# Attention outputs of batches two to four: transposed by TensorE into free PSUM columns instead of by DMA

## The chip, the cores and the metric

The kernel runs on one core of one Trainium2 chip. The metric is the device time of one execution in microseconds; lower is better. The engines of the core are TensorE (PE, with its weight loads PEld), VectorE (DVE), ScalarE (ACT), GpSimd (POOL) and SyncE (SP, which here only issues DMAs). Each works through its own queue in order and waits on semaphores for the others. TensorE writes to PSUM (here four cells of 128 partitions by 1024 float32 values), the others read it from there.

## The reference

A block-sparse attention (four batches, eight heads, 768 positions, head width 64) is followed by a two-layer network on every token.

```python
scores = scale * np.matmul(q, k.transpose(0, 1, 3, 2))
mask = np.abs(blk_i - blk_j) <= window            # blocks of 32, window 1
mask = mask | (blk_i == 0) | (blk_j == 0) | (blk_i == n_blocks - 1) | (blk_j == n_blocks - 1)
for qb in range(n_blocks):
    for kb in sampled_blocks[qb]:                 # three sampled blocks for each block of queries
        mask[qb * block:(qb + 1) * block, kb * block:(kb + 1) * block] = True
attn = softmax(np.where(mask, scores, -1e9))
x = np.matmul(attn, v)        # then heads side by side: 3072 tokens x 512
h = x @ w_in                  # 512 x 2048
r = np.maximum(h, 0.0)
out = (r * r) @ w_out         # 2048 x 512
```

(The softmax is written out in the reference; it is shortened here.)

## The kernel before, in words

**Units and stages.** A unit `u` is a pair of heads of one batch (four units to a batch, `HP = 4`). Batches one and two (`SB = 2`) compute dense scores for tiles of 256 queries (`q0` is 0, 256 or 512), in three pairs of key chunks: `scores`, `exps`, `masks`, then `values` (or `values_full`), which leaves the unnormalized outputs and their sums in one PSUM cell, `otile`. Batches three and four gather only the key and value blocks that are needed. They go by six visits `v` of 128 queries, all four units at once: `s_scores`, `s_exps`, `s_masks`, and `s_values`, which leaves the outputs of all eight heads in one PSUM cell.

**From the outputs to the network.** `normalize` and `s_normalize` (VectorE: a reciprocal and a multiplication) write the outputs as bfloat16, with tokens on the partitions. The network's first matmul (`hidden`) needs them with features on the partitions, in a tile `xT` for each 256 tokens of a batch. Batch one takes the way over TensorE: `normalize` writes `xq`, `x_transp` transposes it by identity matmuls into columns 384 to 511 of the same PSUM cell, which the outputs leave free (`spare_of`), and `x_evac` copies that to `xT`. Batches two to four take the way over DMA: `normalize` and `s_normalize` write to the two-slot tile `XS`, and `x_transp_dma` (two transfers for a tile of batch two) and `s_transp` (one for a visit) issue transposing DMAs from SyncE that write `xT`. There the PSUM cell is given back after the normalization.

**The network.** For each of the twelve tiles of 256 tokens `hidden` is issued in four units `f` of four parts, then `relu` (ScalarE or VectorE) and `square` (ScalarE, GpSimd or VectorE), then eight parts of `output`, `out_copy` and `store`. Hidden and output matmuls of earlier tiles are interleaved with the attention of later ones.

**What sets the order.** `PROGRAM` is a list of words, one for each task, written out by hand or by a planner outside of the kernel: a letter for the engine (P, V, A, G, S), the task's number, and after a slash the PSUM cell of a task that takes one. Tasks are numbered in the order in which the code creates them, so a change in the number of tasks renumbers all later ones. `run_program` issues them in this order, and each engine's queue has its words in the order of the list. `get` and `put` name the buffers that a task takes and gives back. All matmul pairs are recorded at one line (203, in `pair`), and all copies at lines 121 and 123 (in `copy`), so the profile's groups are told apart by tiles and shapes.

Of the kernel before, what the change touches and what calls it, by code (L numbers as in the profile page):

```python
# [19 lines left out]
P = 128  # L20
# [5 lines left out]
def kernel(  # L26
# [11 lines left out]
    nc = tc.nc  # L38
# [12 lines left out]
    QW = 256  # L51
# [348 lines left out]
    def x_claim(b, q0, e):  # L400
        xs_at[0] += 2

    def normalize(u, q0, w, e):
        n = w // P
        po = outs_of(otile[u, q0], w)
        rs = work.tile([P, 2, 2, 1], F32, name="rs", tag="rs")[:, :, 0:n]
        V.reciprocal(out=rs, in_=po[:, :, :, D:VW])
        b, a = divmod(u, HP)
        xq = XS[:, :, a] if b else XQ[buf_of["xq", u, q0].at][:, 0:n]
        V.tensor_tensor(out=xq.rearrange("p c h d -> p h c d"), in0=po[:, :, :, 0:D], in1=rs.broadcast_to([P, 2, n, D]), op=AOP.mult)  # L410
        if not b:
            xtile[u, q0] = xq
        else:
            otile.pop((u, q0))
# [11 lines left out]
    def x_tile(b, c0):  # L426
        if (b, c0) not in xT:
            xT[b, c0] = XTT[xb[b, c0].at]
        return xT[b, c0]
# [4 lines left out]

    def x_transp_dma(b, q0, e):
        for c in range(2):
            sy.dma_start(out=x_tile(b, q0)[:, :, c * P:(c + 1) * P], in_=XS[:, c].rearrange("p a h d -> p (a h d)"), transpose=True)  # L437
# [214 lines left out]
    def s_normalize(b, v, e):  # L652
        po = otile.pop(("s", b, v))[:, :, 0:HP * VW].rearrange("p h (a d) -> p h a d", d=VW)
# [7 lines left out]
    def s_transp(b, v, e):  # L661
        sy.dma_start(out=x_tile(b, v // 2 * QW)[:, :, v % 2 * P:v % 2 * P + P], in_=xtile.pop(("s", b, v)).rearrange("p a h d -> p (a h d)"), transpose=True)
# [115 lines left out]
    def T_(f, *args, **kw):  # L778
        return Task((lambda e: f(*args, e)), **kw)
# [61 lines left out]
    def attend(a, add):  # L841
# [24 lines left out]
        by_dma = b > 0  # L866
        if by_dma:
            if (b, q0) not in x_of:
                xsb = [Buf("xs"), Buf("xs")]
                x_of[b, q0] = (T_(x_claim, b, q0, get=xsb), [], xsb)  # L870
            cl, nms, xsb = x_of[b, q0]
            nms.append(T_(normalize, u, q0, w, deps=[va, cl], put=[ob[u, q0], ot]))
            if len(nms) == HP:
                t = T_(x_transp_dma, b, q0, deps=nms + x_get(b, q0), put=xsb)
                mu.update({(b * HP + i, q0): t for i in range(HP)})
            return
# [5 lines left out]
    def visit(b, v, vw, acts):  # L882
# [28 lines left out]
        nm = T_(s_normalize, b, v, deps=[va], get=[xs], put=[yb, ot])  # L911
        mu["s", b, v] = T_(s_transp, b, v, deps=[nm] + x_get(b, v // 2 * QW), put=[xs])

    x_of = {}
# [46 lines left out]
    for T in TILES:  # L961
# [35 lines left out]
        V109 V153 V207 V332 V18 V19 V20 V28 V42 V53 V294 V29 A32 V35 P30/0 P36/1 P0/2 P33/3 V31 V37 A1 P11/0 V34 P100/1 G46 A101  # L997
        P47/0 P104/2 V43 A105 P44/3 P102/1 V45 V57 V48 A103 P58/2 V54 P111/3 V59 P55/0 A112 P113/2 V56 P115/1 V41 P4/0 A114 P9/3
        P125/0 V67 P2/3 A116 P106/2 V3 G52 G64 A126 P5/3 P123/1 V107 A124 P108 P65/3 G74 P121/0 V110 V66 P68/2 A122 V69 G63 P82/1
        P84/3 P131/2 V83 A85 P135/0 A132 P86/1 P117/3 G49 V87 A136 P10/2 G60 V118 G73 P61/1 P133/2 V62 P90/0 P119 G38 A134 P12/1  # L1000
        V120 V91 P168/1 G75 P15/3 P39/3 P174/0 A169 V40 P127/2 G76 A175 P137/3 G78 V128 P144/1 G70 V138 P129 P147/0 A145 V130 P139
        V176 P88/2 A89 V140 P71/1 V170 P171/3 A148 P779/2 V72 P780 V146 A172 P187/1 P92/0 P781 V93 A188 P782 V173 P50/3 P181/0 A783
        P177/1 V189 V51 A182 P141/2 V178 G784 P772/3 P773 A142 V149 P184/0 P179 P774 G79 G22 V180 A185 P94/2 P775 V143 P155/1 A95
        V776 G785 P150/0 A156 P158/2 V151 P161/3 A159 P786/1 V183 P152 P787 V186 A154 P215/2 A162 P788 V157 P14/0 P789 V160 A216
        P98/0 P190/3 S80 V163 A99 P212/2 V790 A778 P164/0 S251 S252 A213 V191 S81 P793/1 G791 A777 V165 P794 P209/2 P192 G792 P166
        P795 A210 V167 V193 P796 V217 S259 S260 P822/0 G77 V383 A797 P823 P197/3 P194/2 P824 V214 A198 G799 P825 P816/1 A195 V826
        P817 G254 P226/3 A798 P818 S255 V196 A227 P200/2 P810/0 V264 P811 A201 V211 S267 P243/3 P819 V256 S265 P812 A244 V228 P218/2
        V199 P813 A820 P219 P800/3 S257 A814 V220 V202 P240/1 P221 P801 A241 V262 S261 P96/0 S263 P802 A222 V97 A815 P237/1 V242
        P223/2 P203/0 A238 V245 P803 V272 A224 P229/1 P204 S268 P804 A230 V225 S275 S276 P805 A821 V231 S273 P286/2 G266 V205 P806
        A287 P232/1 V239 A827 P206 P289/2 P233 V270 P807 V208 A290 S271 V234 P296/0 A808 V291 P246/2 S253 P235 P247 V236 A297 V288  # L1010
        S437 P299/3 P828/1 V248 P829 A300 V280 P302/0 P830 V278 A303 P249 P283/3 V250 S279 V298 P831 A284 P314/2 P850/0 V832 V434
        S277 P851 A315 S281 P844/3 V304 P845 A833 V285 P311/1 P852 V258 A312 P853 V301 P846 S269 P847 A854 S21 V316 P292/2 V313
        P862/1 A848 P293 P305/0 V295 A855 P863 G282 P308/3 P306 G849 S454 A309 P864 S436 V307 P353/2 P865 A354 P326/3 P856/0 V866
        P857 A327 P320/2 P858 V274 A321 P323/1 V310 S438 P834/3 S445 V355 A324 P859 S444 V322 P347/2 S460 P835 V495 A860 V328 V325
        P317/1 A348 P350/0 P318 P836 S809 A351 V319 V349 P329/2 A867 P334/1 V352 P330 P837 V331 A335 V23 P356/0 S333 A861 P340/2
        P838 G447 A341 P839 G439 P362/1 G441 P357 P840 A363 G459 S452 P337/2 P841 S442 A338 G443 P868/1 G449 A842 V345 P359/2 P869
        S450 A360 P374/3 V342 P870 A375 V358 S446 P365/2 S440 V339 P377/3 A366 P871 V336 A378 V361 P343/0 S843 P371/2 V364 P344 S462
        P872 V367 A372 S448 V346 P368/3 V376 P398/2 P369 V373 A399 P873 S461 V379 S453 P380/0 V370 V469 P401/2 P381 A402 P385/3 V382
        P874 V400 A386 S384 P391/0 P388/2 V451 A392 V403 P16/3 P875 A389 P404/3 V876 P884/0 S612 P885 A405 P425/2 P886 V406 A426
        G463 P24/1 P887 V26 V25 P878/3 A888 P879 P428/2 G467 P880 S630 A429 P881 S468 V427 P407/0 V27 A882 S464 G465 P408 V396  # L1020
        P422/2 A889 V409 P924/1 G455 P925 A423 V457 P926 S456 P890/3 V387 A883 P927 V393 P891 A928 P413/0 V390 P892 P893 A414 S466
        P896/2 V894 P897 A929 P394/1 P898 V424 P395 P416/0 V397 P930/3 S458 A417 G470 A895 S614 P899 G472 P931 S604 V538 V900 P410/1
        S613 P932 A411 S471 P933 V430 P902/0 A934 V501 P475/2 P903 A476 A901 P912/1 V418 P904 V415 S620 V412 P431/3 V497 V540 V477
# [61 lines left out]
```

## Time and profile before

| | us |
|---|---|
| median of 3 runs (lowest, highest) | 256.85 (256.68, 257.36) |
| profiled execution | 254.29 |
| its span, first to last instruction | 252.5 |
| TensorE busy | 240.6 |
| ScalarE busy | 184.3 |
| VectorE busy | 166.0 |
| GpSimd busy | 93.6 |

"Busy" counts an engine's instructions, not its register, branch, semaphore and DMA-issuing ones. A matmul of the table lasts from its issue to its modelled end, and matmuls overlap, so the mean time of one matmul is not what it adds to the queue: that is seen from the start of one row of the timeline to the start of the next. In rows of groups the numbers after the bar are total busy time, mean nanoseconds of one, and idle time of the engine just before them, with what ended it. In rows of waits: total microseconds, times, and the longest. In rows of one line or tile the three durations are the shortest, the median and the longest in nanoseconds.

### The profile page before, as it was taken

Reading aid. Unit: us, or ns where it says so; the run is one execution under the profiler, and the core shown is the slowest. Engines: PE = TensorE matmul, PEld = TensorE weight load, DVE = VectorE, ACT = ScalarE, POOL = GpSimd, SP = SyncE. Lnnn points to the kernel's source line nnn. Section 1 sums busy time; section 2 is a strip of 40 time slices with the busy share of each in tenths; the row PEclk is TensorE's granted clock in tenths of the full one; section 3 lists DMA queues with packets and bytes.
Section 4 is the critical chain, followed back from the end, with each engine's and each line's share of the span. In section 5 each row is a group of like instructions: output and inputs, shape, how many; then the busy total and the mean of one; then the engine's idle time right before and its main releaser. Section 6 shows DMA issues by size and latency. Waiting matters only on the chain.

```text
span 252.5 us, 12042 instructions
## 1 busy us (share of the span) xinstructions
PE 240.6 (95%) x5265; PEld 179.0 (71%) x5265; DVE 166.0 (66%) x394; ACT 184.3 (73%) x216; POOL 93.6 (37%) x192
## 2 busy tenths in 40 slices
PE   7878999999999998999999999999999999999993
PEld 4646889768965677876866875867866765777683
DVE  7657997879789979685474876535566667641301
ACT  3978999999998889768758777768697465235340
POOL 3075525010407005329337982053806307060110
PEclk9999999999999999999999999999999999999999
DMA  6999999999999999995799999951835645242022
GB/s 194 365 243 181 204 188 278 221 275 182 272 280 195 160 253 308 181 248 135 223 301 178 223 238 204 286 132 34 258 56 86 159 125 142 65 127 83 3 86 86
DMA packets 63507, 47.08 MB, mean 186 GB/s; under 512 B 31455, under 2 KB 58464, under 8 KB 63456
## 3 DMA queue, kind: packets, MB, share of 16 engines
q1 hardware_dynamic: 58320, 37.61, 64.3%
q0 software_dynamic: 4448, 8.25, 16.0%
q8 instruction: 41, 0.67, 1.2%
q10 hardware_dynamic: 688, 0.46, 0.6%
q14 instruction: 10, 0.08, 0.1%
HBM read 35.51 MB, written 7.91 MB: 172 GB/s over the span
## 4 chain that ended last, share of the span: by engine, by line
PE 77%; DMA 11%; DVE 5%; ACT 2%; POOL 2%; SPq 1%; issue 1%; DVEq 0%; POOLq 0%; ACTq 0%
PE X L203 70%; PE X L649 5%; DMA xT<-XS 4%; DMA w_out_sb<-in_moe_w_out_dram 3%; DMA KG<-in_k_dram 2%; ACT pT L357 2%; DVE pT L364 1%; PE X L395 1%; DVE r L705 1%; POOL g L716 1%; SPq L169 1%; DMA out_dram<-ys 1%; POOL qc L123 1%; PE X L305 1%; SPq L437 1%
## 5 line engine op out<-in xcount | busy, mean ns | idle before, releaser
L203 PE MATMUL X<-xT,w_in_sb 64*128 64x256 bf16 x1536 | 99.1, 269 | 1.6 <-DMA xT<-XS 1.4
L203 PE MATMUL X<-w_out_sb,g 64*128 64x512 bf16 (+3 forms) x960 | 94.5, 333 | 0.1
L203 PEld LDWEIGHTS <-w_in_sb 64*128 64x128 bf16 x1536 | 73.3, 94 | 14.4 <-issue 2.5
L357 ACT ACTIVATE pT<-X 128x1024 bf16<-128x1024 f32 x72 | 70.7, 1038 | 7.5 <-PE X L203 5.0
L203 PEld LDWEIGHTS <-g 64*128 64x128 bf16 x960 | 39.7, 94 | 26.8 <-issue 0.2
L619 ACT ACTIVATE pT<-X 128x768 bf16<-128x768 f32 (+1 forms) x56 | 41.6, 765 | 22.8 <-PE X L203 21.9
L714 ACT ACTIVATE g<-r 128x1024 bf16<-128x1024 f32 (+1 forms) x44 | 40.3, 932 | 11.8 <-DVE r L705 11.7
L705 DVE TENSOR_SCALAR r<-X 128x1024 f32<-128x1024 f32 x22 | 26.9, 1224 | 25.9 <-PE X L203 23.9
L364 DVE TENSOR_TENSOR pT<-pT,VG 128x1024 bf16<-128x1024 bf16 x60 | 39.5, 694 | 1.8 <-ACT pT L357 1.7
L716 POOL TENSOR_TENSOR g<-r 128x512 bf16<-128x512 f32 (+1 forms) x16 | 20.7, 1305 | 48.7 <-ACT r L703 25.5
L626 DVE TENSOR_TENSOR pT<-pT,MKS 128x768 bf16<-128x768 bf16 (+1 forms) x48 | 28.2, 616 | 12.0 <-ACT pT L619 11.5
L703 ACT ACTIVATE r<-X 128x1024 f32<-128x1024 f32 x26 | 27.5, 1071 | 11.6 <-PE X L203 11.4
L203 PE MATMUL X<-QKT 64*128 64x256 bf16 (+1 forms) x384 | 31.7, 250 | 0.9 <-issue 0.4
L573 POOL DMA_INDIRECT VG<-rows,idx x20 | 20.5, 1025 | 19.4 <-PE X L203 10.2
L123 POOL CAST VB<-vs 128x768 bf16<-128x768 f32 x10 | 8.6, 869 | 34.9 <-DMA vs<-in_v_dram 22.3
L203 PEld LDWEIGHTS <-QKT 64*128 64x128 bf16 x384 | 17.0, 95 | 6.3 <-issue 1.6
L203 PEld LDWEIGHTS <-pT 64*128 64x128 bf16 x768 | 15.4, 94 | 3.4 <-issue 0.2
L203 PE MATMUL X<-VB,pT 64*128 64x65 bf16 x768 | 16.9, 190 | 0.1
L123 POOL CAST qc<-ks 128x384 bf16<-128x384 f32 (+1 forms) x17 | 8.5, 530 | 22.5 <-DMA ks<-in_k_dram 14.8
L203 PEld LDWEIGHTS <-KG 64*128 64x128 bf16 x528 | 12.9, 95 | 4.2
L203 PE MATMUL X<-QKT,KG 64*128 64x64 bf16 x528 | 14.6, 190 | 0.0
L649 PEld LDWEIGHTS <-pT 128*64 128x64 bf16 x624 | 11.6, 111 | 3.0 <-issue 2.7
(104 smaller groups left out, 197.5 us busy)
## 6 DMA issues: line engine op xcount, KB each, us to landing
vs<-in_v_dram SPq DMA_DIRECT2D x14, 384.0 KB
ks<-in_k_dram SPq DMA_DIRECT2D x13, 384.0 KB
qs<-in_q_dram SPq DMA_DIRECT2D x12, 384.0 KB
out_dram<-ys SPq DMA_DIRECT2D x9, 512.0 KB
VG<-rows SPq DMA_DIRECT2D x20, 132.0 KB
w_in_sb<-in_moe_w_in_dram POOLq DMA_DIRECT2D x2, 1024.0 KB, 9.9
w_out_sb<-in_moe_w_out_dram POOLq DMA_DIRECT2D x4, 512.0 KB, 8.9
rows<-VB SPq DMA_DIRECT2D x2, 792.0 KB
```

Source lines behind the costliest of these rows:

```text
L123: (V if e == "DVE" else G).tensor_copy(out=out, in_=in_)
L203: last = nc.tensor.matmul(out(r ^ crossed), lhsT(r ^ crossed, rows), rhs(r ^ crossed, rows), skip_group_check=True, **kw)
L357: A.activation(out=pT[:, :, 0:n], in_=stile.pop(a)[:, :, 0:n], func=AF.Exp, scale=scale)
L364: V.tensor_tensor(out=pT, in0=pT, in1=m[:, None].broadcast_to([P, 2, len(cs), w]), op=AOP.mult)
L573: G.indirect_dma_start(out=to[0:RS * HB], out_offset=None, in_=pairs, in_offset=bass.IndirectOffsetOnAxis(ap=idx[0:RS * HB, g - 1:g], axis=0))
L619: A.activation(out=pT[:, :, 0:n], in_=stile.pop((u, v, gs))[:, :, 0:n], func=AF.Exp, scale=scale)
L626: V.tensor_tensor(out=pT, in0=pT, in1=m[:, None].broadcast_to([P, 2, n]), op=AOP.mult)
L649: nc.tensor.matmul(po[i * D:(i + 1) * D, h, a * VW:(a + 1) * VW], pts[g][:, h, c * D:(c + 1) * D], val, start=a == 0 and c == 0, stop=c == ...
L703: A.activation(out=to, in_=src, func=AF.Relu)
L705: V.tensor_scalar(out=to, in0=src, scalar1=0.0, scalar2=None, op0=AOP.max)
L714: A.activation(out=g, in_=r, func=AF.Square)
L716: (G if e == "POOL" else V).tensor_mul(out=g, in0=r, in1=r)
```

## The change

Batch two takes batch one's way: `normalize` always writes `xq`, and `x_transp` and `x_evac` follow. For batches three and four `s_transp` becomes a TensorE task with eight transposes (four units, two row halves) into the spare columns of the visit's PSUM cell, and a new task `s_evac` copies them to `xT`. The cell is given back by `s_evac` (batch two: `x_evac`) instead of by the normalization. The 18 transposing DMAs and `x_claim` go. Not touched are the 24 DMA transposes of queries and keys (`transp_dma`).

```diff
     def normalize(u, q0, w, e):
...
-        xq = XS[:, :, a] if b else XQ[buf_of["xq", u, q0].at][:, 0:n]
+        xq = XQ[buf_of["xq", u, q0].at][:, 0:n]
...
-    def x_transp_dma(b, q0, e):
-        for c in range(2):
-            sy.dma_start(out=x_tile(b, q0)[:, :, c * P:(c + 1) * P], in_=XS[:, c].rearrange("p a h d -> p (a h d)"), transpose=True)
...
     def s_normalize(b, v, e):
-        po = otile.pop(("s", b, v))[:, :, 0:HP * VW].rearrange("p h (a d) -> p h a d", d=VW)
+        po = otile["s", b, v][:, :, 0:HP * VW].rearrange("p h (a d) -> p h a d", d=VW)
...
     def s_transp(b, v, e):
-        sy.dma_start(out=x_tile(b, v // 2 * QW)[:, :, v % 2 * P:v % 2 * P + P], in_=xtile.pop(("s", b, v)).rearrange("p a h d -> p (a h d)"), transpose=True)
+        xs, pt = xtile.pop(("s", b, v)), spare_of(otile["s", b, v], HP * P)
+        for a in range(HP):
+            for r, rows in enumerate(HALVES):
+                nc.tensor.transpose(pt[:, r, a], xs[rows, a].rearrange("p h d -> p (h d)"), identb[rows, rows])
+
+    def s_evac(b, v, e):
+        to = x_tile(b, v // 2 * QW)[:, :, v % 2 * P:v % 2 * P + P]
+        copy(e, to.rearrange("r a (h p) -> r h a p", h=2), spare_of(otile.pop(("s", b, v)), HP * P))
...
-        by_dma = b > 0
-        if by_dma:
...
-            return
         xqb = buf_of["xq", u, q0] = Buf("xq")
...
-        nm = T_(s_normalize, b, v, deps=[va], get=[xs], put=[yb, ot])
-        mu["s", b, v] = T_(s_transp, b, v, deps=[nm] + x_get(b, v // 2 * QW), put=[xs])
+        nm = T_(s_normalize, b, v, deps=[va], get=[xs])
+        xt = T_(s_transp, b, v, deps=[nm], put=[xs])
+        mu["s", b, v] = T_(s_evac, b, v, deps=[xt] + x_get(b, v // 2 * QW), put=[yb, ot])
```

The diff also replaces the whole of `PROGRAM` (1,222 words before, 1,252 after). Beside the new tasks and the renumbering, the list has another order from its beginning, with other engines for some tasks that the change does not touch. How many tasks of a kind each engine has, where the two lists differ:

| task | before | after |
|---|---|---|
| `x_evac` | 10 VectorE, 2 ScalarE | 14 VectorE, 10 ScalarE |
| `s_evac` | none | 10 VectorE, 2 ScalarE |
| `relu` | 22 VectorE, 26 ScalarE | 19 VectorE, 29 ScalarE |
| `square` | 44 ScalarE, 16 GpSimd | 32 ScalarE, 16 GpSimd, 12 VectorE |
| `k_gather` | 11 GpSimd, 11 VectorE | 17 GpSimd, 5 VectorE |
| `v_gather` | 20 GpSimd, 2 SyncE | 14 GpSimd, 8 SyncE |
| `cast_qk` | 20 GpSimd, 16 VectorE, 1 ScalarE | 21 GpSimd, 13 VectorE, 3 ScalarE |
| `cast_v` | 12 GpSimd, 4 VectorE | 9 GpSimd, 5 VectorE, 2 ScalarE |
| `mask_evac` | 5 VectorE, 4 ScalarE | 6 VectorE, 3 ScalarE |
| `mask_rows_evac` | 1 VectorE, 1 ScalarE | 2 ScalarE |
| `evac` | 13 VectorE | 12 VectorE, 1 ScalarE |
| `out_copy` | 6 VectorE, 9 ScalarE | 7 VectorE, 8 ScalarE |

129 lines of the change are left out of this document (58 added, 71 removed).

## The prediction

> **What bounds the kernel now.** I read the engines' totals first, then the same by stretches of the span, then the waits of TensorE, and only then the chain.
>
> ```profile
> span 252.5 us, 12042 instructions
> PE 240.6 (95%) x5265; PEld 179.0 (71%) x5265; DVE 166.0 (66%) x394; ACT 184.3 (73%) x216; POOL 93.6 (37%) x192
> PEclk9999999999999999999999999999999999999999
> ...
> 9.50:20.00 10.50, 8.61 (x185) 6.65 (x186) 6.54 (x17) 8.52 (x10) 6.22 (x10) 1.00 1.00 282
> ...
> 20.00:60.00 40.00, 39.09 (x854) 32.05 (x853) 33.92 (x71) 38.84 (x47) 11.99 (x22) 1.00 1.13 223
> 60.00:90.00 30.00, 29.96 (x714) 21.90 (x710) 26.60 (x68) 27.34 (x30) 7.94 (x12) 1.00 1.07 230
> 90.00:120.00 30.00, 28.32 (x619) 21.39 (x615) 22.46 (x56) 24.99 (x30) 13.53 (x38) 1.00 1.01 215
> 120.00:150.00 30.00, 30.00 (x710) 22.37 (x707) 20.64 (x49) 20.95 (x26) 19.13 (x41) 1.00 1.04 228
> 150.00:160.00 10.00, 9.39 (x196) 6.57 (x190) 5.28 (x8) 7.53 (x9) 3.17 (x3) 1.00 1.21 208
> 160.00:247.00 87.00, 87.00 (x1838) 62.45 (x1836) 43.48 (x104) 50.66 (x63) 29.64 (x55) 1.00 0.43 116
> ```
>
> The columns are length, then busy time (and count) of PE, weight loads, DVE, ACT and POOL, the granted clock and the DMA share. From 20 to 247 us TensorE is idle for 0.91 + 0.04 + 1.68 + 0 + 0.61 + 0 = 3.24 us of 227. Between 9.5 and 20 us it idles another 1.89. So it is the bound nearly everywhere, at a granted clock of 1.00, and whatever is put on it lengthens the span unless it falls into one of those gaps. DVE and ACT are nearly full until 90 us (ACT 38.84 of 40) and have room after it.
>
> The transposing DMAs stand large in the chain, and this needs care:
>
> ```profile
> PE 77%; DMA 11%; DVE 5%; ACT 2%; POOL 2%; SPq 1%; issue 1%; DVEq 0%; POOLq 0%; ACTq 0%
> ...
> 93.37 5.36 DMA xT<-XS
> ...
> 152.21 5.56 DMA xT<-XS
> ...
> PE X L203 <- DMA xT<-XS: 1.4, 2, 0.8
> ...
> 98.86 2.38 PE L203 MATMUL X<-xT,w_in_sb 64*128 64x256 bf16 x36 [0.77 <-DMA xT<-XS]
> ...
> 157.90 1.05 PE L203 MATMUL X<-xT,w_in_sb 64*128 64x256 bf16 x16 [0.60 <-DMA xT<-XS]
> ```
>
> Two transfers of 5.4 and 5.6 us are on the chain, 10.9 us together. But TensorE worked on other tiles while they ran: what it lost is the last two rows, 0.77 and 0.60 us, and the list of waits gives the same 1.4 us in two places. That, not 10.9 us, is what the transposing DMAs cost on the path.
>
> **What is removed.** The 18 DMAs:
>
> ```profile
> L658 DVE TENSOR_TENSOR XS<-X,ss x12: 691/691/695, 122.7 to 221.7; 128x512 bf16<-128x512 f32 x12
> L662 SPq DMA_TRANSPOSE xT<-XS x12: 1189/1444/2162, 129.0 to 222.4; - x12
> L437 SPq DMA_TRANSPOSE xT<-XS x6: 1202/1514/2987, 75.5 to 117.1; - x6
> its engine sat idle before it (us, times) until:
>   DMA xT<-XS: 0.5, 1
> ```
>
> SyncE gets back 12 x 1.444 + 6 x 1.514 = 26 us of issuing, and loads, window reads and stores queued behind a transpose no longer wait for its normalization. No row shows TensorE waiting for those loads after 30 us, so I give this nothing; in the new order it is partly spent again, because six more gathers of batches three and four (eight instead of two, six transfers each) are issued by SyncE and six fewer by GpSimd. Gain on the path: the 1.4 us of waits. DVE's one wait of 0.5 us for a buffer of XS was not on TensorE's path.
>
> **What is added on TensorE.** In batch two, 12 tiles with 4 transposes each; in batches three and four, 12 visits with 8 each: 48 + 96 = 144, or 36 groups of four. Batch one already does the same operation, in the same form (64 rows, 64 columns, two row halves side by side):
>
> ```profile
> L424 PE MATMUL X<-identb,xq x48: 188/190/200, 13.2 to 59.2; 64*128 64x64 bf16 x48
> its engine sat idle before it (us, times) until:
>   DVE xq L410: 0.8, 2
> ...
> 54.12 0.54 PE L203 MATMUL X<-VB,pT 64*128 64x65 bf16 x24
> 54.49 0.23 PE L424 MATMUL X<-identb,xq 64*128 64x64 bf16 x4
> 54.55 0.40 PE L203 MATMUL X<-QKT 64*128 64x256 bf16 x4
> 54.77 0.54 PE L203 MATMUL X<-VB,pT 64*128 64x65 bf16 x24
> 55.13 1.05 PE L203 MATMUL X<-w_out_sb,g 64*128 64x512 bf16 x8
> 55.99 0.40 PE L203 MATMUL X<-QKT 64*128 64x256 bf16 x4
> ...
> 19.45 0.08 PE X L424 x4
> ```
>
> One transpose takes 190 ns, but the instructions are pipelined: the group begins at 54.49 and the next matmul at 54.55, so four transposes move the queue by 0.06 us; the chain gives 0.08 for a group that something waited for. 36 x 0.06 = 2.2 us, 36 x 0.08 = 2.9 us. I take 2.3, since most groups stand in the middle of the queue as this one does.
>
> [...] What a whole batch of such groups does to the clock no run here shows.
>
> **What is added on VectorE and ScalarE.** 24 copies out of PSUM, 12 of 128x256 and 12 of 128x512:
>
> ```profile
> L123 DVE COPY xT<-X 128x256 bf16<-128x256 bf16 x10 | 2.8, 288 | 0.9 <-PE X L424 0.9
> L121 ACT COPY xT<-X 128x256 bf16<-128x256 bf16 x2 | 0.7, 366 | 0.0
> L123 DVE COPY QKT<-X 128x512 bf16<-128x512 bf16 x4 | 1.7, 420 | 0.7 <-PE X L305 0.7
> L121 ACT COPY ys<-X 128x512 f32<-128x512 f32 x1 | 0.6, 586 | 3.4 <-PE X L203 3.4
> L407 DVE RECIPROCAL rs<-X 128x4 f32<-128x4 f32 x24 | 4.3, 180 | 6.7 <-PE X L203 5.3 <-PE X L395 1.3
> L655 DVE RECIPROCAL ss<-X 128x8 f32<-128x8 f32 x12 | 2.5, 208 | 12.5 <-PE X L649 10.3 <-PE X L203 1.7 <-ACT g L714 0.4
> ```
>
> The wide ones cost 10 x 0.42 on VectorE and 2 x 0.59 on ScalarE, 5.4 us over batches three and four, where from 120 to 247 us VectorE is idle for 57 us. Batch two's cost 4 x 0.29 and 8 x 0.37, 4.1 us; ScalarE is idle for 7.7 us from 60 to 120. These run beside TensorE and I cost them at nothing. Their cover is TensorE's hidden-layer and output matmuls, which need no PSUM cell from the tile being copied; without it each would show with its whole length.
>
> **The waits that the change adds.** A transpose is in TensorE's in-order queue, and waits for VectorE's reciprocal and multiplication: 0.18 + 0.42 us in batch two, 0.21 + 0.69 in batches three and four. Everything that stands behind it on TensorE waits too, and then ScalarE, which lives on scores. Reading the new order, the tightest place in batch two is the last unit of the first query tile: between its values and its transposes stands only one eighth of an output tile, 8 matmuls that move the queue by 0.86 us (55.13 to 55.99), against 0.60 needed. In batches three and four the tightest has some 1.2 us against 0.90. So it fits if VectorE is free, and VectorE has mask multiplications and relus in its queue. The nearest rows for the size are batch one's: 12 tiles lost 0.8 us. Bounds for 24 tiles: 0 and 1.6 us. I take 0.5, as VectorE has more room after 120 us. The PSUM cell of a tile is also held on through the transposes and the copy; below nothing this cannot go, and the same 1.6 covers it.
>
> **What the new order moves besides.** The whole list of instructions is arranged anew. Until the last exponential of batch one ScalarE gets two casts, one more mask row, one copy and one relu more, and one mask tile and two half squares fewer: by rows of like shape about +0.9 us, where it has 1.16 idle of 40. Bounds 0 and 0.9; I take 0, since hidden-layer matmuls stand between and TensorE needs no exponential for them. Later ScalarE loses 12 squares to VectorE and GpSimd takes 6 key gathers from VectorE: both away from the bound, nothing on the path.
>
> **Sum.** +2.3 transposes, -1.4 waits for DMAs, +0.5 new waits: +1.4 us. On the profiled execution (254.29 us, span 252.5) that is 255.7 and 253.9. The median of the runs is 256.85, so 258.3 us.
>
> **Rivals.** *Faster, through the junctions of the batches.* Between 90 and 120 and between 150 and 160 us the DMA waits were not all that TensorE lost: 1.68 + 0.61 = 2.29 us against 1.4. If the short way through PSUM lets hidden-layer work start early enough to fill these gaps, and the start loses 0.9 us less of its 1.89, then 2.3 - 2.29 - 0.9 = -0.9: 256.0 us. For it: the 5.4 us latency goes. Against it: ScalarE and VectorE are full up to there, and one keep-warm filler still stands at that place in the new list. It decides if the stretch from 90 to 120 us idles under 0.3 us.
> *No change:* the gaps fill but the start does not improve: 2.3 - 2.29, about 256.9.
> *The tiles' wait becomes the bound:* transposes at 2.9, waits at 1.6, ScalarE's 0.9 on the path: 2.9 - 1.4 + 1.6 + 0.9 = +4.0, 260.9 us. For it: VectorE at 34 of 40 and ScalarE at 38.8 of 40 in the first stage. Against it: after 120 us neither is near full.
> *The transposes do not overlap with the rest:* 72 pairs at their full 190 ns are 13.7 us, 270 us. [...]
>
> **How the numbers follow.** Forecast 0.46, its own range 257.7 to 259.4; faster 0.22; no change 0.16; the tiles' wait 0.14; no overlap 0.02. A measurement of this kernel tells about 0.3% (0.8 us) from nothing. Faster 0.22, same 0.16, slower 0.46 + 0.14 + 0.02 = 0.62. The range goes from a little under the faster case, 255.6, to the bound of the third, 261.0.
>
> **What would show it.** The profile after should have no transfer that writes xT, 192 transposes in two groups of lines at 190 ns, TensorE's busy time up by 2 to 3 us, and the waits of 0.77 and 0.60 us gone. From 120 to 247 us the work should end about 2 us later in its place, with no new gap over 0.5 us. I am wrong if TensorE's idle time from 20 to 247 us is above 5 us (the waits are bigger) or under 1 us (the gaps filled), or if the clock falls.

## The result, and the profile after

The changed kernel takes 268.75 us in the median (266.74 to 270.12, four runs) against 257.11 us for the kernel before, run beside it: 1.0475 times as long, with a 95% interval of 1.0418 to 1.0532. Two later sets on other chips gave 1.0464 (1.0393 to 1.0535) and 1.058 (1.0366 to 1.0793). The profiled execution took 268.26 us, its span is 266.4 us, 13.9 us longer than before's. Before's profile is of an execution of 254.29 us, faster than all four of its timed runs (256.68 to 258.43), so some 2 to 3 of the 13.9 us are the choice of that execution: by the medians the loss is 11.6 us. (A ratio leaves out the runs that the chip made in a second, slower state, and a median does not, so the two need not agree to the last digit.) Before's runs spread over 252.5 to 262.4 us in the last set, which makes its intervals wide; the prediction had taken 0.8 us as the least difference to be told from nothing.

The page's totals, then TensorE by the same stretches as in the prediction (length, then busy time and count of PE, weight loads, DVE, ACT, POOL, the granted clock, the DMA share):

```profile
span 266.4 us, 12451 instructions
PE 246.8 (93%) x5409; PEld 184.4 (69%) x5409; DVE 175.4 (66%) x370; ACT 182.5 (69%) x221; POOL 108.4 (41%) x229
PEclk9999999999999998899999999999999999889999
```

```profile
9.50:20.00 10.50, 8.31 (x184) 6.75 (x186) 6.34 (x17) 8.79 (x10) 7.36 (x19) 1.00 0.94 280
20.00:60.00 40.00, 37.11 (x819) 28.82 (x815) 32.21 (x66) 35.71 (x41) 12.31 (x14) 1.00 1.09 212
60.00:90.00 30.00, 28.50 (x632) 21.56 (x628) 26.41 (x65) 27.61 (x33) 11.23 (x13) 1.00 0.99 272
90.00:120.00 30.00, 27.85 (x643) 21.93 (x637) 24.58 (x44) 22.35 (x28) 16.97 (x36) 0.94 0.81 175
120.00:150.00 30.00, 29.61 (x702) 22.10 (x698) 21.58 (x47) 20.49 (x26) 17.23 (x52) 1.00 0.84 176
150.00:160.00 10.00, 9.27 (x236) 6.76 (x236) 7.29 (x12) 6.14 (x7) 6.00 (x10) 1.00 1.02 229
160.00:261.00 101.00, 97.88 (x2072) 70.57 (x2070) 51.32 (x103) 54.57 (x69) 34.32 (x74) 0.98 0.35 99
```

From 9.5 us on, TensorE idles 2.19 + 2.89 + 1.50 + 2.15 + 0.39 + 0.73 + 3.12 = 12.97 us; the same sum before was 1.89 + 3.24 = 5.13. That is 7.8 of the 13.9 us. The granted clock, 1.00 throughout before, falls in two places. Finer windows (same columns) hold two steps at half clock, some 3.4 us long:

```profile
105.10:108.50 3.40, 3.40 (x48) 2.44 (x42) 3.37 (x8) 1.97 (x2) 0.30 (x1) 0.50 1.29 143
...
231.40:234.80 3.40, 3.40 (x61) 2.06 (x56) 2.28 (x5) 0.35 (x1) 0.00 (x0) 0.50 0.02 5
```

They cost at most 2 x 1.7 = 3.4 us. Idle time, half clock and 36 groups of transposes at 0.06 us (2.2) make 13.4 of the 13.9 us between these two executions. What TensorE waited for, as total, times and longest:

```profile
PE X L418 <- DVE xq L407: 2.5, 5, 0.9
PE X L639 <- DMA VG<-rows: 2.4, 1, 2.4
PE X L203 <- DVE pT L364: 2.1, 1, 2.1
PE X L305 <- POOL qc L123: 2.1, 2, 1.4
```

The first row holds both batch one's transposes, which the change does not touch, and batch two's new ones. Batch one's end at 60.21 us, and four of the five waits lie ahead of that (0.26, 0.23, 0.37 and 0.73 us, 1.6 together, where before lost 0.8). Only one is a wait of a new transpose. It stands at the place that the prediction called the tightest of batch two, the last unit of the first query tile:

```profile
77.54 1.80 DVE L364 TENSOR_TENSOR pT<-pT,VG 128x1024 bf16<-128x1024 bf16 x2
79.47 0.42 DVE L407 TENSOR_TENSOR xq<-X,rs 128x256 bf16<-128x256 f32 x1
79.95 0.23 PE L418 MATMUL X<-identb,xq 64*128 64x64 bf16 x4 [0.88 <-DVE xq L407]
```

VectorE was busy with two mask multiplications, as the prediction had feared, and TensorE lost 0.88 us. Three larger stalls belong to the list's order; each can be followed some way back.

*At 48 us, a cast in front of a normalization of batch one.* From the timeline of all engines, and from SyncE's issues (start, length):

```profile
45.66 0.53 PE L203 MATMUL X<-VB,pT 64*128 64x65 bf16 x24
...
48.13 0.56 DVE L123 CAST qc<-ks 128x768 bf16<-128x768 f32 x1 [3.46 <-DMA QKT<-qc]
48.60 0.18 DVE L404 RECIPROCAL rs<-X 128x4 f32<-128x4 f32 x1
48.81 0.42 DVE L407 TENSOR_TENSOR xq<-X,rs 128x256 bf16<-128x256 f32 x1
49.30 0.23 PE L418 MATMUL X<-identb,xq 64*128 64x64 bf16 x4 [0.73 <-DVE xq L407]
```

```profile
43.37 6.57 SPq L312 DMA_TRANSPOSE QKT<-qc  x2
```

The cast of unit 4's keys (a `cast_qk` that the new list gives to VectorE) is the fifth in a row to want one of four `qc` buffers; the four ahead of it are on GpSimd. It waits 3.46 us until a transposing transfer has emptied a buffer. Behind it in VectorE's queue stands the normalization of the values that TensorE had finished at 46.19 us (first row). It begins at 48.60, some 2.4 us later; TensorE's transposes, batch one's, wait 0.73 us for it. Behind that stand three mask multiplications. In the old list this cast was on GpSimd, and the first of the five.

*At 102 us, a mask multiplication beside GpSimd's square.*

```profile
100.53 3.59 DVE L364 TENSOR_TENSOR pT<-pT,VG 128x1024 bf16<-128x1024 bf16 x3 [1.65 <-ACT pT L357]
100.73 2.25 POOL L713 TENSOR_TENSOR g<-r 128x1024 bf16<-128x1024 f32 x1 [2.79 <-ACT r L700]
...
104.18 0.29 PE L203 MATMUL X<-VB,pT 64*128 64x65 bf16 x8 [2.15 <-DVE pT L364]
```

```profile
L364 DVE TENSOR_TENSOR pT<-pT,VG x60: 675/684/2382, 23.7 to 116.2; 128x1024 bf16<-128x1024 bf16 x60
```

One of 60 mask multiplications takes 2.38 us instead of 0.68, while GpSimd makes a square that the old list had on ScalarE. The values wait for it, and TensorE idles 2.15 us.

*At 228 us, gathers that come late.* SyncE's issues, then TensorE:

```profile
204.41 0.40 SPq L768 DMA_DIRECT2D out_dram<-ys  x1
205.02 9.56 SPq L566 DMA_DIRECT2D VG<-rows  x12
217.49 8.83 SPq L566 DMA_DIRECT2D VG<-rows  x12
226.37 1.26 SPq L541 DMA_DIRECT2D VG<-rows  x2
...
230.12 2.25 PE L639 MATMUL X<-VG,pT 128*64 128x65 bf16 x96 [2.38 <-DMA VG<-rows]
```

Four value gathers (line 566) of six transfers each go out in two rows of twelve, some 0.74 to 0.8 us a transfer, with window reads (line 541) behind them. The last two window reads leave from 226.37 us on, and the values of the last visits wait for them. The gathers also began late: ahead of them in SyncE's queue stood a store that waited 8.8 us, until 204.41, for VectorE's copy of an output tile. How much earlier they would have gone without that store was not measured.

### The profile page after: what moved, and what is told of

It is laid out like the page before. It is cut to its first block, busy times and chain, and to the rows that moved or that the text cites. A ratio compares the mean times of both kernels' runs of the same rounds, so it can differ in the third digit from the quotient of the medians.

```text
span 266.4 us, 12451 instructions
## 1 busy us (share of the span) xinstructions
PE 246.8 (93%) x5409; PEld 184.4 (69%) x5409; DVE 175.4 (66%) x370; ACT 182.5 (69%) x221; POOL 108.4 (41%) x229
## 4 chain that ended last, share of the span: by engine, by line
PE 60%; DMA 10%; DVE 10%; ACT 8%; SPq 7%; issue 4%; POOL 0%; ACTq 0%; DVEq 0%; POOLq 0%
PE X L203 54%; DVE pT L364 6%; ACT pT L357 5%; DMA QKT<-qc 4%; PE X L639 4%; SPq L566 3%; DMA KG<-in_k_dram 2%; DMA qs<-in_q_dram 2%; DVE r L702 1%; DMA VG<-rows 1%; ACT r L700 1%; PE X L395 1%; SPq L546 1%; DVE xq L407 1%; DMA out_dram<-ys 1%
## 5 line engine op out<-in xcount | busy, mean ns | idle before, releaser
L203 PE MATMUL X<-xT,w_in_sb 64*128 64x256 bf16 x1536 | 101.8, 272 | 1.4 <-ACT pT L357 0.7
L713 POOL TENSOR_TENSOR g<-r 128x512 bf16<-128x512 f32 (+1 forms) x16 | 23.8, 1493 | 68.1 <-DVE r L702 38.6
L364 DVE TENSOR_TENSOR pT<-pT,VG 128x1024 bf16<-128x1024 bf16 x60 | 42.6, 759 | 3.3 <-ACT pT L357 3.2
L700 ACT ACTIVATE r<-X 128x1024 f32<-128x1024 f32 x29 | 31.0, 1072 | 16.8 <-PE X L203 16.5
L711 ACT ACTIVATE g<-r 128x1024 bf16<-128x1024 f32 (+1 forms) x32 | 28.6, 906 | 5.7 <-DVE r L702 5.5
L616 DVE TENSOR_TENSOR pT<-pT,MKS 128x768 bf16<-128x768 bf16 (+1 forms) x48 | 24.2, 539 | 11.6 <-ACT pT L609 9.9
L702 DVE TENSOR_SCALAR r<-X 128x1024 f32<-128x1024 f32 x19 | 23.2, 1220 | 12.8 <-PE X L203 12.8
L584 POOL COPY KG<-QKT 128x64 int32 x102 | 25.9, 299 | 0.0
L123 DVE COPY ys<-X 128x1024 f32<-128x1024 f32 (+1 forms) x7 | 7.6, 1090 | 14.2 <-PE X L203 14.2
L563 POOL DMA_INDIRECT VG<-rows,idx x14 | 14.1, 1010 | 6.5 <-issue 4.6
```

The source lines that it names most:

```text
L123: (V if e == "DVE" else G).tensor_copy(out=out, in_=in_)
L203: last = nc.tensor.matmul(out(r ^ crossed), lhsT(r ^ crossed, rows), rhs(r ^ crossed, rows), skip_group_check=True, **kw)
L364: V.tensor_tensor(out=pT, in0=pT, in1=m[:, None].broadcast_to([P, 2, len(cs), w]), op=AOP.mult)
L563: G.indirect_dma_start(out=to[0:RS * HB], out_offset=None, in_=pairs, in_offset=bass.IndirectOffsetOnAxis(ap=idx[0:RS * HB, g - 1:g], axis=0))
L584: eng.tensor_copy(out=rows[:, :, :, r_ * w:(r_ + 1) * w], in_=src[:, :, :, bass.ds(at[r_] * w, w)])
L616: V.tensor_tensor(out=pT, in0=pT, in1=m[:, None].broadcast_to([P, 2, n]), op=AOP.mult)
```

## The experiments

The theory after the result: most of the loss belongs to the new list (places as the three above, with the half-clock steps behind two of them), not to the transposes. The rivals: the transposes and their copies cost it, by holding PSUM cells and TensorE's queue; or the half clock costs it, and comes from the transposes. In what follows "the old order" is the list of before with the new tasks added.

**Transposes in the old order, at a first try.** The 24 transposes and 24 copies stand right behind their normalizations, and the PSUM cells are dealt anew.

```diff
 list of before
-S x_transp_dma, S s_transp
+P x_transp, V x_evac; P s_transp, V s_evac   (each behind its normalization)
```

> The transposes alone: the list of the kernel before is kept, with its engines; only the 18 transposing DMAs are taken out and the 36 groups of TensorE transposes (144) and 24 copies put in, each group about 1.0 us (batch two) or 1.3 us (batches three and four) of TensorE work behind its values, and the PSUM cells dealt out again. Theory A (the transposes and their waits cost the time: about +11.6 us): 266 to 270 us. Theory B (the new order costs it, and the transposes cost 2.3 us of TensorE less the 1.4 us of waits for DMAs): 257.5 to 260 us.

Measured: 264.56 us, 1.0318 (1.023 to 1.0407). The waits of its profile are now for cells that still hold scores:

```profile
PE X L203 <- ACT pT L357: 3.4, 7, 0.9
```

The time lies between the ranges of both theories. With a careless placing the change loses 3% even in the old order; this run says nothing yet about a good one.

**The transposing DMAs in the new order.**

```diff
 changed list
-P x_transp, x_evac; P s_transp, s_evac
+S x_transp_dma, S s_transp   (where the last copy of a tile or visit stood)
```

> The new order alone: the list of the kernel after with its engines, but the outputs of batches two to four transposed by the 18 DMAs as before; the 144 transposes and 24 copies are left out of the list and the DMAs stand where the last copy stood. Theory A: about 257 us. Theory B: 265 to 268 us, with the same two stretches at half clock (near 105 and 231 us of the span).

Measured: 283.8 us, 1.0979 (1.0872 to 1.1086), outside both ranges. Its profile is of a run of 286.96 us:

```profile
PE X L203 <- DMA xT<-XS: 17.7, 6, 6.6
```

Six waits for transfers take 17.7 us: the new list uses `xT` so soon after it is made that the transfers come too late. The run doesn't price the order by itself and is inconclusive for that.

**The gathers back on GpSimd.** One of the net six gathers as an example; the number is the task's.

```diff
-S517  v_gather
+G517  v_gather
...
-G737  v_gather
+S737  v_gather
```

> The kernel after, with the value gathers of batches three and four issued by the engines of the kernel before (2 instead of 8 by SyncE, 20 instead of 14 by GpSimd). If the late gathers on SyncE make the idle stretch of 2.4 us near 228 us and the half clock for 3.4 us after it, 4.1 us go (2.4 + 3.4 / 2): 264.7 us, and the half-clock stretch near 231 us is gone. If the gathers only move another wait into view: over 267 us.

Measured: 266.17 us, 1.0392 (1.0316 to 1.0467), 2.6 us less than the changed kernel's median in its first set, and between the two forecasts. The wait for `VG<-rows` at 228 us and the half-clock step behind it are gone; the stall at 102 us and its step are still there.

**The square back on ScalarE.**

```diff
-G919  square(1, 0, 256), columns 4 to 8
+A919  square(1, 0, 256), columns 4 to 8
```

> The kernel after, with one square of 128x1024 (second unit of the first tile of batch two, 2.25 us on GpSimd at 100.7 us) on ScalarE as before. If this square slowed the mask multiplication beside it on VectorE from 0.69 to 2.38 us and so made TensorE idle for 2.15 us and then run at half clock for 3.4 us, 2.15 + 1.7 = 3.9 us go, less up to 1.0 us for ScalarE: 265 to 266 us, and the half-clock stretch near 105 us is gone. If the slow multiplication has another cause: 268 to 270 us.

Measured: 267.8 us, 1.0449 (1.0364 to 1.0534). That is 1 us less than the changed kernel's median, but its runs (266.71 to 268.67) and the changed kernel's (266.74 to 270.12) overlap, so no gain is shown. The long multiplication is gone:

```profile
L364 DVE TENSOR_TENSOR pT<-pT,VG x60: 673/685/996, 23.0 to 115.3; 128x1024 bf16<-128x1024 bf16 x60
```

This shows the square as its cause, and the half-clock step near 105 us is gone with it. But TensorE's waits in the same profile name another place, which the first profile of the changed kernel did not have:

```profile
PE X L203 <- DMA QKT<-qc: 2.6, 1, 2.6
```

This wait for transposed queries and keys is not the work of the edit alone: it lies at 61 us, ahead of the square, and the unchanged kernel has 1.8 us of it in its third profile. It comes and goes between executions, and here it hid what the repair may have gained.

**Without the transposes of batches two to four.** A pair of small matmuls on constants, of 64 or 128 columns, takes the place of a tile's or visit's transposes, so that it need not read what the normalization writes. The copies stay, so `xT` holds something else.

```diff
     def s_transp(b, v, e):
-        xs, pt = xtile.pop(("s", b, v)), spare_of(otile["s", b, v], HP * P)
-        for a in range(HP):
...
+        xtile.pop(("s", b, v))
+        pair(lambda i: otile["s", b, v][:, i, 384:512], lambda i, rows: warm[rows, 0:P], lambda i, rows: warm[rows, 0:P], start=True, stop=True)
```

> The kernel after with the 144 transposes of batches two to four left out: in place of each group one pair of constant matmuls (64 columns in batch two, 128 in batches three and four) fills the spare columns, so that the copies and the longer hold of the PSUM cells stay, while TensorE does about 1.0 instead of 2.2 us there and waits for no normalization. If the transposes and their waits cost the time (Theory A): 258 to 261 us. If copies, hold and the new order cost it: 2.2 - 1.0 for the work and about 1.5 us for the waits less, 266 us.

Measured: 272.4 us, 1.0512 (1.0416 to 1.0607), where before took 258.84 us. Its profile limits what this run says:

```profile
82.54 0.20 PE L203 MATMUL X<-warm 64*128 64x64 bf16 x2 [0.73 <-DVE xq L407]
```

One pair still waits 0.73 us for a normalization, at the place where the changed kernel lost 0.88, so this wait was not taken out as the text on record says. And TensorE idles 3.6 us on "issue", that is, for nothing that the profile shows; the first and the third profile of the changed kernel have none of that. The changed kernel was not run on this chip; its ratios elsewhere are 1.0464 to 1.058. So no gain is seen from leaving the transposes' own work out, which speaks against the rival that they cost the loss; what settles it is the comparison in the old order below.

**Every transpose twice, in the new order.**

```diff
-        for a in range(HP):
+        for a in [*range(HP)] * 2:
```

> The kernel after with each of the 36 groups of transposes issued twice. At 0.06 us for each four (0.12 for each eight) it is 2.2 us longer: 271 us. If a transpose costs TensorE its full latency (190 ns for each pair, 13.7 us for all), about 282 us.

Measured: 275.05 to 282.83 us in four runs (median 280.12), too far apart for a price. It was measured again in the old order below.

**Both repairs.** The edits of the two repairs together.

> The kernel after with both repairs at once: the value gathers on the engines of the kernel before, and the one square on ScalarE. If the two stalls with their half-clock stretches are separate and add up: 268.75 - 4.1 - 3.9 = 261 us by the profile, 265 us by the medians of the two repairs alone (2.6 and 1.0 us). No stretch at half clock should be left before the end.

Measured: 272.76 us, 1.0554 (1.0476 to 1.0631), on the chip on which the kernel without transposes ran. Neither of the two stalls is in its profile, and yet the ratio is within the changed kernel's on other chips (1.0464 to 1.058). Its profile has other idle time, 2.9 us of transposes that wait for normalizations and 4.0 us on "issue". So the two repairs do not add up, and it stays open whether the stalls that they remove were the bulk of the loss or were replaced by others.

**Filling the idle time at 228 us.** 45 more pairs of keep-warm matmuls ahead of the values of visit 4 of batch four.

```diff
+    for _ in range(45):
+        wb = Buf("X")
+        T_(keep_warm, wb, get=[wb], put=[wb])
```

> The kernel after with 45 pairs of constant matmuls (2.4 us of TensorE work whose result is overwritten) just ahead of the values that wait for the late gathers near 228 us. TensorE is no longer idle there, while the gathers land when they did. If the half clock follows from the idle stretch, the stretch near 231 us at half clock goes and 1.7 us with it: 267 us. If the clock falls for another reason, or the filler only delays: 268.5 to 271 us.

Measured: 274.89 us, 1.0591 (1.05 to 1.0682). In its profile, of the longest of its four runs (277.71 us), the gathers landed later still and TensorE idled 2.83 us behind the filler, with no half-clock step after it. Inconclusive.

**Transposes in the old order, placed with care.** As the first try, but the cells of before are kept up to batch two, and each group stands some matmuls behind its normalization.

> The transposes alone again, in the list of the kernel before, with its PSUM cells kept up to the first tile of batch two and each group of transposes and each copy placed by hand so that fewer tasks wait for a cell. If most of the 7.5 us of the first such kernel were cells held too long at bad places: 258 to 260 us, or 1.005 to 1.012 of the kernel before on the same chip. If the hold of the cells costs that much wherever they stand: 263 to 265 us, 1.025 to 1.03.

Measured: 260.56 us against 258.04, 1.0105 (1.0039 to 1.0172). A second time, in another set (its text stands further on): 261.55 against 258.47, 1.0145 (1.0103 to 1.0187). The page of the second:

```profile
span 258.5 us, 12303 instructions
PE 246.7 (95%) x5409; PEld 186.4 (72%) x5409; DVE 172.3 (67%) x409; ACT 188.1 (73%) x225; POOL 96.4 (37%) x192
```

The same 5409 matmuls as in the changed kernel, in a span that is 7.9 us shorter. By the medians the transposes alone cost 2.5 and 3.1 us, by the ratios 1.05% and 1.45%, 2.7 and 3.7 us; the intervals go from 1.0 to 4.8 us.

**The same with every group of batches two to four twice.**

> The kernel with the placed transposes, with each of the 36 groups of batches two to four issued twice. At 0.06 us for each four it is 2.2 us over the placed kernel on the same chip (at 0.08 us 2.9); with no overlap 13.7 us over it.

Measured: 266.81 us, 1.0349 (1.0292 to 1.0405): 6.25 us for 36 more groups. Their own cost is seen in the timeline, from the start of one row to the start of the next: 16 transposes move TensorE's queue by 142.30 - 142.07 = 0.23 us,

```profile
142.07 0.40 PE L655 MATMUL X<-identb,XS 64*128 64x64 bf16 x16
142.30 1.03 PE L203 MATMUL X<-w_out_sb,g 64*128 64x512 bf16 x8
```

and eight in the changed kernel by 0.11:

```profile
177.76 0.28 PE L655 MATMUL X<-identb,XS 64*128 64x64 bf16 x8
177.87 1.03 PE L203 MATMUL X<-w_out_sb,g 64*128 64x512 bf16 x8
```

That is 0.06 us for a group of four, 2.2 us for 36, as predicted. But the whole kernel lost 6.25 us, and the forecast of 2.2 to 2.9 us missed. The two profiles show some of the rest: TensorE idles 15.5 us of the span where the placed kernel idles 12.6, half of the difference between 90 and 105 us, and the half clock ahead of 15 us lasts 6.83 us where it lasts 3.41 there. Why, was not found out.

**The changed kernel again**, as the control of this set.

> The kernel after, unchanged, on this chip beside the others: 1.04 to 1.055 of the kernel before. If it comes out at 1.06 or more on a chip where the four kernels of the last comparison did too, chips differ in how late the transfers land, and the new order is the more sensitive to it.

Measured: 269.98 us, 1.0464 (1.0393 to 1.0535), within the forecast. This is the plainest comparison of all: on one chip and in one set the same tasks took 260.56 us in the old order (1.0105) and 269.98 in the new one. Order, engines and cells alone cost 9.4 us.

Its profile, and that of a third measurement further on, tell which stalls recur. Those at 102 and 228 us do, with 2.1 and 2.4 to 2.5 us in all three. The one at 48 us does not: here the cast, at 49.35 us, waits for no buffer and the transposes behind it wait for nothing. This execution lost time elsewhere, 2.4 us at 23 us in a wait for weights (`w_in_sb`) with 6.83 us of half clock, and was no shorter.

**Transposes only where a DMA was waited for.** The kernel before, with TensorE transposes for the tile of batch two and the visit of batch three whose transfers TensorE waited for (0.77 and 0.60 us).

```diff
-        by_dma = b > 0
+        by_dma = b > 0 and (b, q0) not in PEX     # PEX = ((1, 256),), and visits PES = ((2, 2),)
```

> The kernel before with TensorE transposes only where TensorE waited for a DMA: the second query tile of batch two (four groups) and the third visit of batch three (one group of eight); the other 15 DMAs stay. Added 6 x 0.06 = 0.4 us, the 1.4 us of waits gone: 1.0 us less than the kernel before, 0.996 of it. If the waits go elsewhere: within 0.3% of it or up to 1.01.

Measured: 258.94 us, 1.0077 (1.0027 to 1.0126). The waits for those transfers are gone from the profile, but the kernel is not faster. What took the gain is not shown. The profile has 1.91 us of idle time at 143 us, in the middle of one part of a tile's hidden-layer matmuls:

```profile
141.30 1.92 PE L203 MATMUL X<-xT,w_in_sb 64*128 64x256 bf16 x31 [0.18 <-issue]
145.13 1.14 PE L203 MATMUL X<-xT,w_in_sb 64*128 64x256 bf16 x17 [1.91 <-issue]
```

It waits for nothing that the profile shows. Idle time of this kind is in the profiles of several kernels, and between executions of the changed kernel it is 0, 2.9 and 0 us, so it cannot be charged to the edit.

**Splitting the new list by stretches.** Old and new list contain nearly the same set of tasks in their first 410 words (one task differs) and in their first 800 (five differ). So a list can follow the old order up to there and the new one behind it:

```diff
 words 1 to 410 (or 1 to 800) of the old order
-words behind them, old order
+the other words, in the order and with the engines of the changed list
```

> The transposes stay; the first 410 words of the list are in the old order (to about 66 us, the middle of batch two), all behind them in the new order with its engines. If the loss of the new order lies in its later part (the mask multiplication behind GpSimd's square, the gathers on SyncE, the half-clock steps behind both), this is near the changed kernel: 1.035 to 1.047 times before. If it lies in the first 66 us (casts, squares and mask rows on other engines), it is near the old order with transposes: 1.010 to 1.020.

> As the one before, with the first 800 words in the old order (to about 140 us, the second visit of batch three). Four net value gathers go to SyncE behind that place. If the gathers and the half-clock step behind them are the larger part, 1.025 to 1.035 times before; if the stretch from 66 to 140 us is, 1.010 to 1.018. From the progress of the two profiles (visit 2 of batch three 6.3 us later in the changed kernel, the end 7.6 us later) I expect the second.

> As the one before, with all value gathers on the engines that the old list gives them. If the late gathers cost what the waits of the changed kernel show (2.4 us of idle time and 1.7 us of half clock), it is 2.5 to 4 us faster than the one before and within 1 us of the old order with transposes. If SyncE's issue does not matter in this order, the two are within 1 us.

> The transposes in the old order throughout, again, as the control of this set: 1.010 times before as measured (1.004 to 1.017).

| order, one chip | us | ratio to before |
|---|---|---|
| old throughout | 261.55 | 1.0145 (1.0103 to 1.0187) |
| new from about 140 us, gathers as in the old | 263.33 | 1.0182 (1.0088 to 1.0277) |
| new from about 140 us | 264.54 | 1.0221 (1.0144 to 1.0298) |
| new from about 66 us | 265.08 | 1.0227 (1.0132 to 1.0323) |

(Before: 258.47.) The new order behind 66 us costs 3.5 us by the medians, nearly all of it behind 140 us: my expectation, that the stretch from 66 to 140 us was the dear one, missed. The gathers on SyncE are 1.2 us of it, less than expected. The intervals of neighbouring rows overlap, so single steps of about 1 us between rows are not shown; that the last row is slower than the first is (264.12 to 266.15 against 260.31 to 263.57 us, without the one slowest of all). The kernel that is new from 66 us on has both long stalls, 2.6 us for `VG` and 2.4 for the mask multiplication, and yet only some 40% of the loss beyond the old order. The rest had to lie ahead of 66 us, where no wait of TensorE in the first profile of the changed kernel is longer than 1.4 us.

**The start alone.** The first 295 words in the new order (to the ninth tile of batch one), all others in the old; and the changed kernel beside it.

> The transposes stay; the first 295 words are in the new order with its engines (to the ninth tile of batch one, about 48 us), all behind them in the old order. If the start costs what the last set leaves for it, 1.03 to 1.04 times before; if the start costs only the 2.6 us by which that tile is late in the two profiles (49.3 against 46.7 us), 1.020 to 1.027; if nothing, 1.010 to 1.015. I expect the second.

> The changed kernel again, as the control on this chip: 1.046 to 1.048 times before as measured twice.

Measured: 264.31 us, 1.0351 (1.0135 to 1.0568), and for the changed kernel 269.44 us, 1.058 (1.0366 to 1.0793), both against 258.15. My expectation, 1.020 to 1.027, missed. The windows of the old order, then of the new start:

```profile
9.50:20.00 10.50, 9.81 (x201) 7.81 (x202) 7.32 (x19) 9.80 (x11) 6.44 (x10) 0.93 1.06 293
20.00:30.00 10.00, 9.34 (x198) 7.99 (x199) 8.54 (x21) 9.41 (x12) 4.57 (x9) 1.00 1.13 197
30.00:40.00 10.00, 10.00 (x212) 8.89 (x209) 9.08 (x18) 9.63 (x14) 4.58 (x13) 1.00 1.09 249
40.00:50.00 10.00, 10.00 (x212) 7.95 (x210) 8.10 (x15) 9.97 (x12) 1.69 (x2) 1.00 1.20 194
```

```profile
9.50:20.00 10.50, 9.39 (x178) 7.66 (x179) 7.21 (x18) 9.01 (x10) 7.94 (x20) 0.84 0.88 265
20.00:30.00 10.00, 8.72 (x194) 7.39 (x195) 7.70 (x19) 9.46 (x12) 3.90 (x5) 1.00 1.13 208
30.00:40.00 10.00, 9.97 (x216) 8.57 (x214) 8.93 (x19) 9.03 (x12) 4.38 (x4) 1.00 1.22 220
40.00:50.00 10.00, 8.81 (x184) 6.76 (x180) 6.51 (x11) 8.72 (x11) 4.32 (x6) 1.00 0.83 227
```

TensorE idles 0.69 + 0.66 + 0 + 0 = 1.35 us in the one and 1.11 + 1.28 + 0.03 + 1.19 = 3.61 in the other: 2.3 us more, of which 1.2 us is the place at 48 us. The lower clock of the first row, 0.84 against 0.93, is another 0.9 us; whether it comes from the order is not known. The VectorE row at 48 us is the changed kernel's again, while the old order casts keys at that time without a wait:

```profile
48.12 1.00 DVE L123 CAST qc<-ks 128x768 bf16<-128x768 f32 x1 [3.34 <-DMA QKT<-qc]
```

```profile
47.03 0.55 DVE L123 CAST qc<-ks 128x768 bf16<-128x768 f32 x1
```

By medians the new start costs 264.31 - 258.15 = 6.2 us, less the 2.5 to 3.1 us of the transposes: 3.1 to 3.7 us. The ratio gives more, 3.5% or 9 us with the transposes, and its interval reaches down to 1.0135, which leaves next to nothing; the 2.3 us of idle time speak for the lower of these prices. What the one cast, put back on GpSimd, would mend was not tried.

**The account, by medians.** Transposes in the old order 2.5 to 3.1 us. New order up to some 48 us, 3.1 to 3.7. New order behind 48 or 66 us, 5.1 (269.44 - 264.31) or 3.5 (265.08 - 261.55). The first two are one measured difference of 6.2 us, and with the 5.1 of the same set they make the whole 11.3 us by arithmetic, which tests nothing. With the 3.5 us of the other set they make 9.7 of the 11.3 to 11.9 us that the changed kernel lost in the three sets, so some 2 us are left for the words between 48 and 66 us and for differences between chips. None of the kernels beats the one before.

## Why the prediction was wrong

**"+2.3 transposes": right, as the queue's own time.** 0.06 us a group holds in the changed kernel (0.11 us for eight) and in the doubled one (0.23 for sixteen). What such groups do to the clock, which the prediction left open: nothing that is seen, for in both profiles of the old order with transposes it is 1.00 in every stretch from 20 to 247 us.

**"-1.4 waits for DMAs": the rows went, the gain did not come.** In the old order with transposes TensorE waits for the copies out of PSUM instead, which the prediction cost "at nothing" because hidden-layer matmuls would cover them:

```profile
PE X L203 <- DVE xT L123: 0.8, 2, 0.4
PE X L203 <- ACT xT L121: 0.5, 1, 0.5
```

They take 1.3 us in the profile shown, 0.9 in the other of the same list. With the copies at 1.3 the transposes' sum is 2.2 - 1.4 + 1.3 + 0.2 (the next term, as measured) = 2.3 us, where 2.5 to 3.7 were measured.

**"+0.5 new waits": within its bounds of 0 and 1.6.** New transposes waited 0.2 us in the old order and 0.9 in the changed kernel, there at the place that the prediction had named as the tightest. "It fits if VectorE is free": it was not, because of two mask multiplications. Batch one's transposes, which are no part of this term, waited 1.6 us where they had waited 0.8, half of it for the cast at 48 us: that belongs to the next term.

**"What the new order moves besides": the step that failed.** It said "Bounds 0 and 0.9; I take 0" for the first stage and "both away from the bound, nothing on the path" for the rest. On one chip the order alone costs 9.4 us; by parts the medians give 3.1 to 3.7 us to the start and 3.5 to 5.1 us to the rest. The step weighed each moved task by its engine's busy total. But the cast that was moved to VectorE did not matter by its 0.56 us: it stood 3.46 us in the queue without a buffer, the normalization behind it came 2.4 us late, and TensorE lost 0.7 us there (0.4 and nothing in the other two profiles of the same kernel). So ScalarE's 0.9 us was the wrong quantity to bound. The named places do not add up to the whole, and which of the moved tasks cost the most stays open.

**The six gathers on SyncE** were named ("partly spent again") and given nothing. Twelve transfers take SyncE 9.56 us, begin behind a store that waited 8.8, and are waited for: 2.4 us of idle time in the profile, 1.2 us (late part) to 2.6 us (whole list) by the runs that put them back. My reason, that no row shows TensorE waiting for loads, spoke of the old order of issue.

**The rivals.** *No overlap*, at 270 us, is nearest to the 268.75 us, and that is chance: its mechanism fell by the 0.06 us a group. *The tiles' wait becomes the bound* gave 260.9 us, from terms that the runs do not make that large. *The junctions* and *no change* fell: the stretch from 90 to 120 us idles 2.15 us, not under 0.3. The two marks set for being wrong, idle time above 5 us from 20 to 247 us and a falling clock, both came true. Both are due to the order for the most part: in the old order with transposes the idle time there is 4.3 and 4.6 us in the two profiles and the clock stays at 1.00.

**The half clock** as a rival of its own: steps came in the changed order without its transposes as well. In the set that is new from 66 us on, a run at a mean clock of 0.997 took 264.12 us and runs at 0.982 to 0.985 took 264.58 to 266.15. So at most 2 us hang on the clock there. That it follows the stalls instead of setting them is argued from the order of time: all but two of the 20 steps between the first 20 us and the end come behind or within a stall of over 2 us.

## What to carry to other kernels

When a change comes with a new instruction order, the order is the change: diff it first, and read for each moved task which buffer or transfer it waits for and what stands behind it in its engine's queue, not how many microseconds it adds to the engine's total. A bound of zero on such a list has to be earned: an engine that is 95% busy, as TensorE was here, has little to gain from another order and much to lose, here 9.4 us. A wait that is read off the trace as removable is a gain only when the next latest thing at that place is known, here a copy in place of a transfer. And one profile is one execution: read which stalls recur in a second one before pricing them.

## What the runs showed of the hardware

- **Half-clock steps.** In most profiles the granted clock falls to 0.50 in steps of 3.41 us or of 6.83, besides the last few microseconds. Before's is 1.00 in every stretch of its span, and the kernel with TensorE transposes in two places, at a mean of 0.999 over 257.3 us, has no room for a step. The two steps of the changed kernel (0.50 from 105.09 to 108.51 us and from 231.38 to 234.80) begin 126.3 us apart, 37 times 3.41 us, and so do those of the kernel that is new from 66 us on (0.50 from 102.8 and from 229.1 us). That all steps lie a whole number of such lengths apart is my estimate from these two pairs. Of 21 idle stretches of TensorE from 2.05 to 2.98 us, fifteen had a step that began within them or up to 1.6 us behind them, and six had none (2.05, 2.16, 2.20, 2.43, 2.57 and 2.83 us). After the first 20 us no shorter stretch had one by itself, but a step came behind four of 0.30 to 0.52 us in a row and one behind 0.67 and 1.20 us. Where the DMAs were put into the new order, gaps of 3.8, 5.5 and 6.6 us were each followed by 6.83 us of half clock, but so were gaps of 2.38 and 2.98 us in other runs. The changed kernel's gap of 2.15 us was followed by half clock, and one of 2.83 us elsewhere was not: what decides it, no run here shows.
- **Idle time without a shown cause.** TensorE idled 1.91 us in the middle of a row of hidden-layer matmuls, for nothing that the profile shows ("issue" in its rows). Profiles of the changed kernel have 0, 2.9 and 0 us of it, the kernel with both repairs 4.0. What it is, no run here shows.
- **GpSimd beside VectorE.** A 128x1024 square on GpSimd (2.25 us) stretched a mask multiplication of bfloat16 tiles from 0.68 to 2.38 us; moving the square away brought the longest back to 0.996 us. How the one slows the other, no run here shows. No GpSimd instruction in these traces reads PSUM: the engines that read it, "the others" of the first section, are VectorE and ScalarE.
- **Issue of small transfers.** SyncE needs 0.74 to 0.8 us for each of the gathers' transfers when twelve go out in a row (9.56 and 8.83 us), against a recorded 0.316 us for the issuing instruction itself.
